# Two more landing places for raw weights in the first chunk, and two more steps whose E part is added by TensorE

## The chip, the cores and the metric

The kernel runs on one core of one Trainium2 chip. The metric is the time of one execution in microseconds (us), as the device reports it; the median of several runs is given. A core has five engines with an instruction queue each: TensorE (PE in the profile, with its weight loads as PEld), VectorE (DVE), ScalarE (ACT), GpSimd (POOL) and SyncE (SP, which here only issues transfers). The engines wait for one another through semaphores. Every engine works through its own queue in order.

## The reference, cut to what matters

```python
batch, seq, dim = (8, 3008, 256)          # x, float32
n_tokens, d_model, d_ff = (24064, 256, 1536)

X = np.fft.fft(x, axis=1)
X = np.fft.fft(X, axis=2)
x = X.real.astype(np.float32).reshape(8 * 3008, 256)

gate = 1.0 / (1.0 + np.exp(-(x @ w_gate)))   # w_gate, w_val: 256 x 1536
val = x @ w_val
return (gate * val @ w_out).astype(np.float32)   # w_out: 1536 x 256
```

The weights are created as float64.

## The kernel before, in words

The Fourier transform is done with matrix products. The transform along the features is merged into the weights: `merge` multiplies a piece of `w_gate` or `w_val` with a cosine and sine table (`ps`, 8 matmul records) and ScalarE copies the result out to `G1` and `G2` (L321, L322). The transform along the sequence gives, for each of the 8 batches, the arrays `pk`, `qk` and one row E (feature 128). So a hidden pre-activation is G1 x pk, plus or minus G2 x qk, plus a term with the row E.

The work behind that is cut into chunks of 252 sequence positions (six for a batch) and a chunk into 12 steps, one for each block of 128 hidden features. Steps are numbered through from 0; chunk 0 is steps 0 to 11. In step i of the main loop the instructions are recorded in this order, and each engine keeps its share of that order (the schedule is manual):

- `front_a(i)`: TensorE writes G1 x pk for gate and value into a PSUM bank `pf`. In the first `N1` steps it also adds the E part, a product of G2 with a tile `e0` that is zero but for its row 0 (`pf<-wqk` in the profile).
- `part(i)`: keeps that half sum in `ae`. Outside of steps `N1` to 11, ScalarE does it (L598). In steps `N1` to 11 VectorE does it and adds the E part by itself, with a per-feature factor `ge` (L601, two instructions). From step 12 on, E is put into the bank by ScalarE before the products (`seed`, L582).
- `gate_a(i - 1)` and `gate_b(i - 1)`: the sigmoids and products of the step before (ScalarE L617, L635; VectorE L622 or L619, L634, L636), and on GpSimd sums of the result, `sf` (L640). L634 is the last reader of `pf`.
- weight work of chunk 0 (below).
- `back`: from step 5 on, five of the fifteen products `po` of the output of an earlier group of three steps. A group g of three feature blocks needs `wf[:, g]`, the forms of the output weights. They are built in three portions by `forms(g)`, on GpSimd for group 0 and on VectorE after it (L357, L360), with copies by ScalarE (L364).
- `front_b(i)`: TensorE adds G2 x qk in the same bank `pf`, which therefore must have been read by `part(i)`.
- `side`: transfers and other things placed at a step by hand.

Of eight PSUM banks five hold `po`. The other three serve `pf` and `ps`, one in effect for `ps` while both are used.

In chunk 0 the weights are still being prepared. They come in 18 pieces of 512 KB, as float64, and are turned into float32 by bit operations. `weight_load(j)` starts the transfer of piece j on SP into a raw place. `weight_parts(j)` is two instructions on ScalarE (L285, L286). `weight_join(j)` is three on VectorE (L295, L296, L298) and one on GpSimd (L300). `weight_use(j)` merges the piece or, for a piece of `w_out`, queues `forms`. `merge` also issues two tiny transfers to fill `ge`. Pieces 0 to 9 (`KEEP = 10`) have places of their own. Pieces 10 to 17 use the buffer of the first batch's x (`x4`) after its last reader: three raw places in turn, so that the load of piece j + 3 waits for the join of piece j, and six places for converted pieces. The steps of joins and uses are written out by hand:

```python
    for j, i in enumerate((0, 1, 2, 3, 4, 5, 6, 7, 9), 9):      # join of piece j in step i
        if i:
            pre.setdefault(i - 1, []).append(lambda j=j: weight_parts(j))
    ...
    for j, i in enumerate((0, 0, 1, 2, 0, 3, 4, 5, 4, 6, 7, 8, 8, 8, 11), 3):   # use of piece j in step i
```

Pieces 4, 7, 11, 15, 16 and 17 are of `w_out`. Piece 11 is the last that the forms of group 1 need.

Of the kernel before, what the change touches and what calls it, by code (L numbers as in the profile page):

```python
# [7 lines left out]
F32 = mybir.dt.float32  # L8
# [73 lines left out]
def kernel(  # L82
# [13 lines left out]
    P = 128  # L96
# [10 lines left out]
    WC = 256  # L107
# [20 lines left out]
    cp = ctx.enter_context(tc.tile_pool(name="cp", bufs=2))  # L128
# [4 lines left out]
    def mm(o, l, r, start, stop):  # L133
        nc.tensor.matmul(o, l, r, start=start, stop=stop, skip_group_check=True)  # L134
# [72 lines left out]
    def table_odd():  # L207
# [9 lines left out]
        for par in range(2):  # L217
# [10 lines left out]
    jobs = [(0, 0), (1, 0), (0, 1), (1, 1), (2, 0), (0, 2), (1, 2), (2, 1), (0, 3), (1, 3), (0, 4), (2, 2),  # L228
            (1, 4), (0, 5), (1, 5), (2, 3), (2, 4), (2, 5)]
    RAW, WS = {}, {}  # L230
    shared = {}
    KEEP = 10

    def weight_load(j):


        w, c = jobs[j]
        src = (moe_w_gate, moe_w_val, moe_w_out)[w]
        src = src[2 * c * P : 2 * (c + 1) * P, :] if w == 2 else src[:, c * WC : (c + 1) * WC]
        src = src.rearrange("(c p) f -> p c f", p=P)  # L240

        def some(n, pool, tag):

            if tag not in shared:
                shared[tag] = pool.tile([P, n * WC], F32, name=f"w{tag}", tag=tag)
            return shared[tag]

        def home(j):

            if j in (0, 1, 2, 3, 5):  # L250
                if j > 2:
                    ws = some(5, pqp, "qk")[:, (j // 5) * 2 * WC : (j // 5 + 1) * 2 * WC]
                    return sp.tile([P, 4 * WC], F32, name="raw", tag="sf"), ws
                t = hp.tile([P, 6 * WC], F32, name="raw", tag="h")
                return t[:, 0 : 4 * WC], t[:, 4 * WC :]
            if j in (4, 6, 9):
                t = wf[:, {4: 1, 6: 2, 9: 3}[j]].rearrange("p m n -> p (m n)")
                return t[:, 0 : 4 * WC], t[:, 4 * WC : 6 * WC]
            t = some(10, cp, "c")
            if j == 7:  # L260
                raw = pqp.tile([P, 4 * WC], F32, name="raw", tag="pk")
                return raw, t[:, 6 * WC : 8 * WC]
            return t[:, 0 : 4 * WC], t[:, 4 * WC : 6 * WC]

        if j < KEEP:
            raw, ws = home(j)
        else:
            both = some(24, xp, "x4").rearrange("p (i n) -> p i n", n=2 * WC)
            r, i = (j - KEEP) % 3 * 2, 6 + (j - KEEP) % 6
            raw, ws = both[:, r : r + 2].rearrange("p a n -> p (a n)"), both[:, i]  # L270
        raw = raw.bitcast(I32).rearrange("p (c f w) -> p c f w", c=2, w=2)
        ws = ws.rearrange("p (c f) -> p c f", c=2)
        WS[j] = ws
        if src.dtype == F32:
            nc.sync.dma_start(out=ws, in_=src)
        else:
            RAW[j] = raw
            nc.sync.dma_start(out=raw.rearrange("p c f w -> p c (f w)"), in_=src.bitcast(I32))

    def weight_parts(j):  # L280

        if j in RAW:
            raw, ws = RAW[j], WS[j]
            lo, hi = raw[:, :, :, 0], raw[:, :, :, 1]
            nc.scalar.activation(ws, hi.bitcast(F32), AF.Abs)  # L285
            nc.scalar.activation(lo, lo.bitcast(U32), AF.Copy, scale=2.0 ** -29)  # L286
# [17 lines left out]
    def weight_use(j, other=None):  # L304
        w, c = jobs[j]
        if w == 2:
            WO[c] = WS.pop(j)
            for g in range(NG):
                if (3 * g + 2) // 2 == c:
                    parts_.extend(forms(g))  # L310
        else:
            merge(WS.pop(j), w, c, other)

    def merge(ws, g, c, other):
        cs = slice(c * WC, (c + 1) * WC)
        ps = bank("ps", other)
        for h in range(2):
            for t in range(2):
                mm(ps[:, h * WC : (h + 1) * WC], dt[:, t, h * HD : (h + 1) * HD], ws[:, t, :],
                   h == 0 and t == 0, t == 1)  # L320
        nc.scalar.copy(G2[:, g, cs], ps[:, WC : 2 * WC])  # L321
        nc.scalar.copy(G1[:, g, cs], ps[:, 0:WC])  # L322
        for f in range(c * WC // P, (c + 1) * WC // P):
            (nc.sync if c else nc.scalar).dma_start(
                out=ge[:, g, f : f + 1], in_=G2[0:1, g, f * P : (f + 1) * P])

    def forms(g):

        w = [WO[f // 2].rearrange("p f (a h j) -> p f h a j", h=2, j=TB)[:, f % 2]
             for f in range(3 * g, 3 * g + 3)]  # L330
        f = wf[:, g].rearrange("p m (a j) -> p m a j", j=TB)
        engine = nc.vector if g else nc.gpsimd

        def one(i):
            return w[i // 2][:, i % 2] if i < 6 else f[:, i - 6]

        def blocks(ij, n):

            i, j = ij[0], ij[-1]
            if i == j:  # L340
                return one(i).unsqueeze(1).to_broadcast([P, n, 4, TB])
            if i >= 6:
                return f[:, i - 6 : j - 5]
            if i // 2 == j // 2:
                return w[i // 2]
            lo = 3 * g + i // 2
            if lo % 2 == 0 and j // 2 == i // 2 + 1:
                return WO[lo // 2].rearrange("p f (a h j) -> p h f a j", h=2, j=TB)[:, i % 2]
            return None

        def sums(lo, hi):
            for x, y, op, to in W_SUMS[lo:hi]:
                n = max(len(x), len(y))
                a, b = blocks(x, n), blocks(y, n)
                op = (ALU.subtract, ALU.add)[op]
                if a is not None and b is not None:
                    engine.tensor_tensor(f[:, to - 6 : to - 6 + n], a, b, op=op)  # L357
                else:
                    for i in range(n):
                        engine.tensor_tensor(f[:, to - 6 + i], one(x[i % len(x)]), one(y[i % len(y)]), op=op)  # L360

        def copies():
            for i, (a, sign) in enumerate(W_COPIES):
                nc.scalar.mul(f[:, 11 + i], one(a), float(sign))  # L364
        return [lambda: (copies(), sums(0, 2)), lambda: sums(2, 4), lambda: sums(4, 6)]
# [204 lines left out]
        nc.sync.dma_start(out=EK[i // NFT], in_=ed[b : b + 1, k0 : k0 + n].to_broadcast([P, n]))  # L570

    PF, AP, Z = {}, {}, {}
    N1 = 5

    def seed(i):

# [7 lines left out]
    def front_a(i):  # L584
        (pk, *_), ks, _, _, fs = cut(i)
        if i < NFT:
            seed(i)
        for g in range(2):
            mm(PF[i][:, g], G1[:, g, fs], pk[:, ks], i < NFT and g == 0, True)
        for g in range(2 if i < N1 else 0):  # L590
            mm(PF[i][:, g], G2[:, g, fs], shared["qk"][:, 4 * WC : 4 * WC + CH], False, True)

    def part(i):

        pqe, ks, n, f, _ = cut(i)
        AP[i] = app.tile([P, 2, CH], F32, name="ae", tag="ae")[:, :, 0:n]
        if not N1 <= i < NFT:
            nc.scalar.activation(AP[i], PF[i], AF.Copy, scale=2.0)  # L598
# [11 lines left out]
    def gate_a(i):  # L610
# [6 lines left out]
        nc.scalar.activation(H[p][:, fh, 0:n], PF[i][:, 0], AF.Sigmoid)  # L617
        if N1 <= i < NFT:
            nc.vector.scalar_tensor_tensor(out=z[:, :, ::-1], in0=AP.pop(i), scalar=2.0, in1=PF[i],  # L619
# [116 lines left out]
    for j in range(2):  # L736
        weight_load(j)
# [3 lines left out]
    for j in range(2, 5):  # L741
        weight_load(j)
    sines = load_table(1, NQ // 2)
    next(sines)
    for j in range(5, 7):
        weight_load(j)
# [4 lines left out]
    def weight_round(*js):  # L751
        for j in js:
            weight_parts(j)
            weight_join(j)
# [24 lines left out]
        then()()  # L779
    nc.scalar.dma_start(out=ed[0:1], in_=PQE[0][2][0:1])  # L780
    nc.vector.tensor_copy(e0[0:1], PQE[0][2][0:1, 0:CH])
    weight_parts(9)
    for j in range(KEEP, KEEP + 3):
        weight_load(j)
    weight_use(2)

    per = NFT * len(chunks)
# [2 lines left out]
    def at(i, *fs):  # L790
        side.setdefault(i, []).extend(fs)


    pre, use = {}, {}
    for j, i in enumerate((0, 1, 2, 3, 4, 5, 6, 7, 9), 9):
        if i:
            pre.setdefault(i - 1, []).append(lambda j=j: weight_parts(j))
        pre.setdefault(i, []).insert(0, lambda j=j: weight_join(j))
        if KEEP <= j < len(jobs) - 3:
            at(i, lambda j=j: weight_load(j + 3))  # L800
    for j, i in enumerate((0, 0, 1, 2, 0, 3, 4, 5, 4, 6, 7, 8, 8, 8, 11), 3):
        use.setdefault(i, []).append(lambda j=j: weight_use(j))
    at(N1 - 1, lambda: nc.vector.tensor_copy(PQE[0][1][0:1, 0:CH], PQE[0][2][0:1, 0:CH]))

# [38 lines left out]
    for i in range(count):  # L843
        front_a(i)
        if N1 <= i < NFT:
            part(i)
        if i:
            gate_a(i - 1)
        if not N1 <= i < NFT:
            part(i)  # L850
# [10 lines left out]
        n = 3 if i >= count - 8 else 2 + i % 2  # L861
# [60 lines left out]
```

## Time and profile before

| | |
|---|---|
| time, median of 4 runs | 1967.46 us (1965.06 to 1969.84) |
| time of the profiled execution | 1970.47 us |
| its span, first to last instruction | 1968.6 us |
| mean granted TensorE clock | 0.992 |
| chunk 0 on TensorE, first to twelfth `pf` | 50.26 to 105.12 us |

In the profile, L134 is the line of the helper that records every matmul, so TensorE's rows are told apart by what they write and read: `pf<-pk`, `pf<-wqk` (the E part), `pf<-qk`, `ps`, `po`. `x4` behind a row is a count of records, not a tile. A row's idle time stands in brackets, with the instruction that ended it. A matmul's end is modelled and lies a little behind the next one's start, so pieces of a list are measured from start to start. Rows of the engines' timelines give start and duration in us.

### The profile page before, as it was taken

The page shows a single profiled execution, that of the slowest core. Times are in us where ns is not written, and L with a number is a line of the kernel's source. Part 1 is how long each engine was busy: PE and PEld are TensorE (multiplying, and loading weights), DVE is VectorE, ACT ScalarE, POOL GpSimd, SP SyncE. Part 2 cuts the span into 40 slices and gives each one's busy share as a digit, 9 for nine tenths or more (in the row PEclk, how much of TensorE's full clock was granted, in tenths as well). Part 3 has the DMA queues.
Part 4 walks back from the last instruction along what each step waited for, and adds up shares of the span by engine and source line. Part 5 has one row for each costly group of instructions (what it writes and reads, how often), then busy time and mean ns, then how long its engine had stood idle before and what let it go on. Part 6 is the DMA issues. An engine that isn't in the chain of part 4 may idle for free.

```text
span 1968.6 us, 34539 instructions
## 1 busy us (share of the span) xinstructions
PE 1922.0 (98%) x11252; PEld 1792.0 (91%) x11252; DVE 1569.8 (80%) x3271; ACT 1341.5 (68%) x3124; POOL 1641.2 (83%) x2851
## 2 busy tenths in 40 slices
PE   6999899999999999999999999999999999999997
PEld 4889789998999999999999999999999999999997
DVE  6888797887788877878777887788878887777777
ACT  3567656665777767776777767777677776777775
POOL 3779897997889978897889978998788996777776
PEclk8999999999999999999999999999999999999999
DMA  8361413112112120221113121221210110011011
GB/s 268 89 133 24 102 42 109 47 20 78 22 46 51 22 78 14 52 54 47 46 19 76 24 78 20 45 55 20 79 21 14 19 22 14 14 20 22 14 19 28
DMA packets 169746, 96.78 MB, mean 49 GB/s; under 512 B 133858, under 2 KB 161636, under 8 KB 167020
## 3 DMA queue, kind: packets, MB, share of 16 engines
q1 hardware_dynamic: 167596, 94.02, 20.0%
q8 instruction: 90, 1.47, 0.3%
q10 hardware_dynamic: 1940, 0.56, 0.2%
q14 instruction: 88, 0.72, 0.1%
q0 software_dynamic: 32, 0.00, 0.0%
HBM read 69.83 MB, written 46.71 MB: 59 GB/s over the span
## 4 chain that ended last, share of the span: by engine, by line
PE 89%; DVE 4%; POOL 4%; ACT 1%; DMA 1%; issue 1%; SPq 0%; DVEq 0%; ACTq 0%; POOLq 0%
PE pf L134 47%; PE po L134 39%; POOL sf L640 3%; PE ev L134 2%; PE od L134 1%; DMA x<-in_xf_dram 1%; DVE c L687 1%; DVE h L636 0%; PE ps L134 0%; DVE st L485 0%; POOL x L388 0%; ACT z L635 0%; POOL x L407 0%; POOL x L386 0%; DVE z L622 0%
## 5 line engine op out<-in xcount | busy, mean ns | idle before, releaser
L640 POOL TENSOR_TENSOR sf<-h 128x168 f32<-128x168 f32 (+1 forms) x960 | 553.6, 595 | 201.6 <-DVE h L636 201.5
L640 POOL TENSOR_TENSOR sf<-h,sf 128x168 f32<-128x168 f32 (+1 forms) x1152 | 661.9, 594 | 59.4 <-DVE h L636 59.4
L134 PE MATMUL pf<-qk,G 128*128 128x252 f32 (+1 forms) x2304 | 584.0, 376 | 7.7 <-ACT ae L598 5.6
L134 PE MATMUL pf<-pk,G 128*128 128x252 f32 (+1 forms) x2304 | 584.6, 376 | 0.0
L636 DVE TENSOR_TENSOR h<-z 128x252 f32<-128x252 f32 (+1 forms) x576 | 303.5, 527 | 329.9 <-ACT z L635 329.3
L582 ACT ACTIVATE pf<-ek,ge 128x252 f32<-128x252 f32 (+1 forms) x1128 | 531.6, 471 | 18.4
L134 PE MATMUL po<-sf,wf 128*128 128x168 f32 (+1 forms) x3072 | 530.6, 306 | 0.0
L598 ACT ACTIVATE ae<-pf 128x504 f32<-128x504 f32 (+1 forms) x569 | 335.5, 590 | 238.7 <-PE pf L134 238.2
L687 DVE TENSOR_TENSOR c<-c 128x168 f32<-128x168 f32 (+1 forms) x949 | 485.3, 542 | 5.5 <-ACT c L664 0.3
L134 PEld LDWEIGHTS pf<-pk,G 128*128 128x128 f32 x2304 | 437.0, 190 | 53.5 <-issue 2.3
L134 PEld LDWEIGHTS po<-sf,wf 128*128 128x128 f32 x3072 | 473.5, 190 | 8.3
L134 PE MATMUL po<-h,wf 128*128 128x168 f32 (+1 forms) x2688 | 476.6, 306 | 0.4 <-DVE wf L357 0.4
L134 PEld LDWEIGHTS po<-h,wf 128*128 128x128 f32 x2688 | 428.3, 190 | 17.5 <-DVE wf L357 0.6
L134 PEld LDWEIGHTS pf<-qk,G 128*128 128x128 f32 x2304 | 410.3, 190 | 35.6 <-ACT ae L598 7.6
L622 DVE TENSOR_TENSOR z<-ae,pf 128x504 f32<-128x504 f32 (+1 forms) x569 | 377.8, 664 | 21.0 <-ACT h L617 20.4
L617 ACT ACTIVATE h<-pf 128x252 f32<-128x252 f32 (+1 forms) x576 | 218.3, 379 | 159.4 <-PE pf L134 149.7
L635 ACT ACTIVATE z<-z 128x252 f32<-128x252 f32 (+1 forms) x576 | 231.6, 402 | 98.2 <-DVE z L622 77.0
L634 DVE TENSOR_TENSOR h<-h,pf 128x252 f32<-128x252 f32 (+1 forms) x576 | 232.3, 403 | 0.0
L640 POOL TENSOR_TENSOR sf<-sf 128x168 f32<-128x168 f32 (+1 forms) x192 | 111.6, 581 | 15.1
L640 POOL TENSOR_TENSOR sf<-sf,h 128x168 f32<-128x168 f32 (+1 forms) x192 | 108.0, 563 | 0.0
L134 PE MATMUL ev<-st,x 63*128 63x189 f32 (+3 forms) x372 | 79.3, 362 | 15.2 <-DVE x L388 8.6
L134 PEld LDWEIGHTS ev<-st,x 63*128 63x128 f32 (+1 forms) x372 | 65.2, 197 | 25.7 <-DVE x L388 9.0
(138 smaller groups left out, 906.7 us busy)
## 6 DMA issues: line engine op xcount, KB each, us to landing
x<-xr SPq DMA_DIRECT2D x14, 1536.0 KB
out_dram<-os SPq DMA_DIRECT2D x380, 56.0 KB
xr<-in_xf_dram SPq DMA_DIRECT2D x14, 768.0 KB
xr<-in_xf_dram SPq DMA_DIRECT2D x35, 256.0 KB
ek<-ed SPq DMA_DIRECT2D x39, 126.0 KB
out_dram<-os SPq DMA_DIRECT2D x288, 7.0 KB
st<-in_stab_dram SPq DMA_DIRECT2D x4, 1111.9 KB
x<-in_xf_dram SPq DMA_DIRECT2D x2, 1512.0 KB
```

The source lines that it names most:

```text
L134: nc.tensor.matmul(o, l, r, start=start, stop=stop, skip_group_check=True)
L582: nc.scalar.activation(PF[i][:, g], EK[i // NFT], AF.Copy, scale=ge[:, g, f : f + 1])
L598: nc.scalar.activation(AP[i], PF[i], AF.Copy, scale=2.0)
L617: nc.scalar.activation(H[p][:, fh, 0:n], PF[i][:, 0], AF.Sigmoid)
L622: nc.vector.tensor_tensor(z[:, :, ::-1], AP.pop(i), PF[i], op=ALU.subtract)
L634: nc.vector.tensor_tensor(h[:, fh, 0:n], h[:, fh, 0:n], PF.pop(i)[:, 1], op=ALU.mult)
L635: nc.scalar.activation(z[:, 0], z[:, 0], AF.Sigmoid)
L636: nc.vector.tensor_tensor(h[:, fh, n:], z[:, 0], z[:, 1], op=ALU.mult)
L640: nc.gpsimd.tensor_tensor(block(p, dst), block(p, a), block(p, b), op=(ALU.subtract, ALU.add)[op])
L687: engine.tensor_tensor(t[:, dst * R : (dst + 1) * R], *v, op=(ALU.subtract, ALU.add)[op])
```

## The change

- The raw places of pieces 10 to 17 become five: three in `x4`, and two in a new tile `wm`. That tile is the second buffer of the pool `cp`, which the results of an output chunk (`c`) use from the end of chunk 0 on. Pieces 10 and 11 are loaded into `wm`. The load of piece j + 5 follows the join of piece j.
- Piece 9 is fully converted ahead of step 0, and the first half of piece 10 too. Step 0 has the join of piece 10, step 1 that of 11 and step 2 that of 12. Step 3 has none. From piece 13 (step 4) on, the joins stay where they were.
- Piece 11 is used in step 3 and not in step 4, so the forms of group 1 lie in steps 3, 4 and 5, and not in 4, 5 and 6.
- `N1` is 7: TensorE adds the E part in steps 0 to 6, and ScalarE's `part` stays until step 6. The copy of E into row 0 of `qk` (L803), which the `qk` products behind it use, moves from step 4 to step 6.

The changed file has five more lines from L271 on.

```diff
         else:
             both = some(24, xp, "x4").rearrange("p (i n) -> p i n", n=2 * WC)
-            r, i = (j - KEEP) % 3 * 2, 6 + (j - KEEP) % 6
-            raw, ws = both[:, r : r + 2].rearrange("p a n -> p (a n)"), both[:, i]
+            r, ws = (j - KEEP) % 5, both[:, 6 + (j - KEEP) % 6]
+            if r < 2:
+                if r == 0:
+                    shared["more"] = shared.get("more") or cp.tile([P, 10 * WC], F32, name="wm", tag="c")
+                raw = shared["more"][:, r * 4 * WC : (r + 1) * 4 * WC]
+            else:
+                raw = both[:, 2 * r - 4 : 2 * r - 2].rearrange("p a n -> p (a n)")
...
-    N1 = 5
+    N1 = 7
...
-    weight_parts(9)
-    for j in range(KEEP, KEEP + 3):
+    for j in range(KEEP, KEEP + 5):
         weight_load(j)
+    weight_round(9)
+    weight_parts(10)
     weight_use(2)
...
-    for j, i in enumerate((0, 1, 2, 3, 4, 5, 6, 7, 9), 9):
+    for j, i in enumerate((0, 1, 2, 4, 5, 6, 7, 9), 10):
         if i:
             pre.setdefault(i - 1, []).append(lambda j=j: weight_parts(j))
         pre.setdefault(i, []).insert(0, lambda j=j: weight_join(j))
-        if KEEP <= j < len(jobs) - 3:
-            at(i, lambda j=j: weight_load(j + 3))
-    for j, i in enumerate((0, 0, 1, 2, 0, 3, 4, 5, 4, 6, 7, 8, 8, 8, 11), 3):
+        if KEEP <= j < len(jobs) - 5:
+            at(i, lambda j=j: weight_load(j + 5))
+    for j, i in enumerate((0, 0, 1, 2, 0, 3, 4, 5, 3, 6, 7, 8, 8, 8, 11), 3):
         use.setdefault(i, []).append(lambda j=j: weight_use(j))
```

## The prediction

> **What bounds the kernel now.** I read the page's chain of waits first, then TensorE's timeline of chunk 0, then the timelines of the engines that the waits there name.
>
> ```profile
> PE 1922.0 (98%) x11252; PEld 1792.0 (91%) x11252; DVE 1569.8 (80%) x3271; ACT 1341.5 (68%) x3124; POOL 1641.2 (83%) x2851
> PE 89%; DVE 4%; POOL 4%; ACT 1%; DMA 1%; issue 1%; SPq 0%; DVEq 0%; ACTq 0%; POOLq 0%
> ```
>
> TensorE is the bound: busy 98% of the span and 89% of the chain. Anything taken off another engine counts only where TensorE waits for it, and every added matmul counts in full. The edits lie in steps 0 to 7, so TensorE's own list there is what matters (start, us, line, shape, count, and in brackets the idle time before and who ended it):
>
> ```profile
> 68.41 1.01 PE L134 MATMUL pf<-pk,G 128*128 128x252 f32 x4
> 69.25 1.01 PE L134 MATMUL pf<-wqk,G 128*128 128x252 f32 x4
> 70.11 1.89 PE L134 MATMUL ps<-wf,dt 128*128 128x256 f32 x8
> 71.83 1.01 PE L134 MATMUL pf<-qk,G 128*128 128x252 f32 x4
> 72.68 1.01 PE L134 MATMUL pf<-pk,G 128*128 128x252 f32 x4
> 75.14 1.97 PE L134 MATMUL ps<-wx,dt 128*128 128x256 f32 x8 [1.44 <-ACT G L322]
> ...
> 81.29 1.97 PE L134 MATMUL ps<-wx,dt 128*128 128x256 f32 x8 [0.68 <-ACT G L322]
> ...
> 86.89 1.97 PE L134 MATMUL ps<-wx,dt 128*128 128x256 f32 x8 [0.51 <-POOL sf L640]
> ...
> 95.82 1.01 PE L134 MATMUL pf<-pk,G 128*128 128x252 f32 x4
> ...
> 103.38 1.95 PE L134 MATMUL pf<-qk,G 128*128 128x252 f32 x4 [2.00 <-DVE ae L601]
> ```
>
> The first four lines are step 4, 72.68 begins step 5, 95.82 begins step 9. From 53 to 73.5 us TensorE never waits. In steps 5, 6 and 7 it waits once each, always in front of the weight product ps. Step 10 has a wait of its own. Now who is late (DVE, then ACT):
>
> ```profile
> 72.08 0.76 DVE L295 TENSOR_SCALAR wx<-wx 128x512 f32<-128x512 f32 x1
> 72.88 0.65 DVE L296 TENSOR_SCALAR wx<-wx 128x512 int32<-128x512 int32 x1
> 73.56 1.67 DVE L298 SCALAR_TENSOR_TENSOR wx<-wx 128x512 int32<-128x512 int32 x1
> ...
> 75.76 1.39 DVE L360 TENSOR_TENSOR wf<-wf,wx 128x128 f32<-128x128 f32 x1
> 77.07 0.62 DVE L803 COPY qk<-ek 1x252 f32<-1x252 f32 x1
> 77.61 0.85 DVE L601 SCALAR_TENSOR_TENSOR ae<-ek,ge,pf 128x252 f32<-128x252 f32 x2
> ```
> ```profile
> 73.23 0.68 ACT L285 ACTIVATE wx<-wx 128x512 f32<-128x512 f32 x1 [1.72 <-DMA wx<-in_moe_w_val_dram]
> ...
> 74.36 0.36 ACT L321 COPY G<-ps 128x256 f32<-128x256 f32 x1
> ```
>
> Two causes. ACT waits 1.72 us for piece 14, whose load left SP only at 69.27, when POOL had freed its raw place; behind it in ACT's order stands the copy that empties ps of step 4, and the next ps needs that bank. And DVE has, in step 4, a join (72.08 to 75.15) and the first forms of group 1 (to 77.07), then the copy and the E part: without a pause from 70.40 to 79.4. ACT's z (L635) waits for DVE's L619, and the next copies out of ps stand behind that: 0.68 and 0.51.
>
> **The change part by part, TensorE.** Start to start, from rows with no wait before: pk 0.85 (68.41 to 69.25), E part 0.85, ps 1.73, five products po 1.43 (88.69 to 90.12), qk 0.85. Steps 5 to 8 without waits would be 4 x (0.85 + 1.73 + 1.43 + 0.85) = 19.44. They took 95.82 - 72.68 = 23.14, so 3.70 is lost: 2.63 of idle in the three brackets, about 0.16 more at each (a row's end lies 0.16 behind the next start: 1.01 against 0.85), and 0.6 in slower rows just behind the waits. The change adds the E part to steps 5 and 6: 2 x 0.85 = 1.70 on the bound engine, nothing hides it. If all three waits go: 19.44 + 1.70 = 21.14, that is 2.00 less. If none goes: 1.70 more.
>
> **Do the waits go?** DVE's rows, start to start: gate (L622, L634, L636) 0.59 + 0.34 + 0.34 = 1.27; a join beside a busy POOL 2.31 (80.89 to 83.20); forms of group 1: 1.92, 1.03 (79.86 to 80.89) and 0.96 (85.46 to 86.42); E part 0.78; copy 0.54. New loads against TensorE's step: step 3, 1.27 + 1.92 = 3.2 (of 4.28); step 4, 1.27 + 1.03 + 2.31 = 4.6 (4.28); step 5, 1.27 + 0.96 + 2.31 = 4.5 (5.71); step 6, 1.27 + 2.31 + 0.54 = 4.1 (5.71); step 7, 0.78 + 1.27 + 2.31 = 4.4 (4.86). Before, step 4 alone asked for 1.27 + 3.07 + 1.92 + 0.54 + 0.78 = 7.6. The debt of 0.3 after step 4 is paid in step 5. If that cover failed, a late L634 would hold the pf bank of the second next step, 5 us later: not reached. ACT gets back 2 x 0.49 (L598) in steps 5 and 6; its parts, 2 x 0.57, and the copy out of ps follow with over 2 us to spare before the next ps. The copy of E into qk (now behind step 6) waits for TensorE's last qk of that step; queued behind it on DVE is only the E part of step 7, which needs pk of step 7 anyway (0.85 later, the copy takes 0.54): nothing.
>
> **Loads.** Pieces 10 and 11 need no longer wait for the folded x (SP stood until 48.42) and go out behind piece 9, whose issue ended at 31.67. Pieces 12 to 14 leave at 48.42 as 10 to 12 did, so 14 is there 20 us before ACT wants it; 15 to 17 wait for POOL's joins of 10, 11, 12. On SP they push only the tiny ge transfers, first read by DVE in step 7 (near 85) and sent before 74. What lies ahead of 10 and 11 is the risk:
>
> ```profile
> 45.20 0.68 ACT L285 ACTIVATE wc<-raw 128x512 f32<-128x512 f32 x1 [3.50 <-DMA raw<-in_moe_w_out_dram]
> ```
>
> This is piece 7, and from here DVE runs without a pause to the E copy (L781) that TensorE waits for at 52.05. Pieces 5, 6, 7 left SP within 1.5 us (26.23 to 27.74) and were there at 37.5, 40.1 and 45.2: they came in the order of issue, not together. So I take 0 for two transfers behind them; the other end is sharing, 1.05 MB at 280 GB/s = 3.7 us later, one for one on the path. Earlier than now is excluded, since nothing ahead of them is removed. The Trainium skill, DMA: Bandwidth & Descriptors, section on queues, rings and completion order, says that an engine takes its ring's descriptors in order but that completions need not follow it; by that, too, the sum keeps 0 but not for certain.
>
> Piece 9 is converted where it was (DVE 51.92 to 53.43). Piece 10 follows: ACT 49.35 to 50.5, before the 53.20 at which it next waits; DVE 53.4 to 55.0 (alone) or 56.4 (slowed by POOL, as L296's 1.40 at 68.14 against 0.43 at 59.19), before the 56.68 at which it next works; POOL 1.25, which moves the forms of group 0 to end at 59 to 61, needed at 76. If 10 lands late, ACT has until 52.4 before qk of step 0 moves. Zero, up to 1 for a late landing. A rule that speaks against this: the skill's SBUF — State Buffer, two separate sides, says that VectorE and GpSimd lock each other out of a shared port pair for a whole instruction. By it each of six moved DVE instructions could stand behind one of POOL's 0.73 to 1.3 us; by the rows only some do, and 1.7 us of idle time (55.0 to 56.68) takes that.
>
> **Step 10.** In step 9 DVE still has the join of piece 17 and forms of group 2 (99.14 to 102.47), the same instructions in the same order. The wait of 2.00 stays, and behind it the clock falls: the windows of 2 us from 102 show 0.88, 0.50, 0.77, and eight pf matmuls take 3.64 in place of 1.70, 1.94 lost. I take no change; the ends are 4.1 gained (wait, 0.16 and slow matmuls all gone) and 2 lost (one more such drop).
>
> **Sum.** +1.70 - 3.70 = -2.00. The profiled execution took 1970.47 (span 1968.6), 3.0 above the median of the runs; its like would be 1968.5, and the median goes from 1967.46 to 1965.5. A measurement of this kernel tells about 0.2% (3.9 us) from no change, so the likeliest case lies within that.
>
> **Rivals.** *Stalls of step 10 go as well.* DVE comes to step 8 about 0.9 us earlier (join 16 kept it until 92.8, pk was there at 92), and the clock drops on a wait of 2.00 but not on one of 1.44; a slightly shorter or differently placed wait may keep it. -2.0 with 1.9 to 4.1 more: 1961.4 to 1963.5. Against it: DVE waited for TensorE at 96.87, so nothing older than step 9 is in this wait. *The early loads hold up piece 7*: slower. 3.7 us at 45.20 go to TensorE's wait at 52.05; that wait, 0.8 now, is then over 4, and the clock falls as in step 10 (1.9). 3.7 + 1.9 - 2.0 = +3.6; with 10 late as well, up to 1 more: 1971.1 to 1972.1. It decides from 2 us of delay. Against it: the order of landings. *The waits move instead of going*, to another bank or engine, and the matmuls stay: up to +1.7, 1969.2.
>
> **How the numbers follow.** Likeliest 0.44 (0.04 of it below 1963.5), step 10 too 0.31 (0.29 below), loads hold up piece 7 0.17 (0.14 above 1971.4, smaller delays within), waits move 0.08 (0.02 above). Faster 0.33, same 0.51, slower 0.16. The likeliest alone: 1963.0 to 1967.5. The range reaches to the one rival's 1961.0 and most of the way to the other: 1970.5.
>
> **What would show it.** Right: 28 matmul rows of the E part (pf<-wqk) in place of 20, no wait before ps in steps 5 to 7, ACT without a wait for wx in step 4, pk of step 9 near 93.8, and the wait of 2 us in step 10 still there. Wrong: piece 7 on ACT later than 45.2, a wait at 52 above 1 us, a new wait of pf for a bank or of DVE for ge, or step 10 without its slow matmuls.

## The result, and the profile after

The changed kernel takes 1964.56 us (median of 48 runs, 1961.99 to 1973.79). The kernel before, on the same chips, takes 1967.17 us (72 runs, 1963.89 to 1977.36). The ratio is 0.9984, with a 95% interval of 0.9978 to 0.999: 2.0 to 4.3 us less, 3.1 in the middle (the two medians lie 2.61 apart). That is below the 0.2% that the prediction called no change, with the interval reaching a little past it. The profiled execution of the changed kernel took 1964.89 us (span 1963.0, mean granted clock 0.994).

Its page, TensorE's share of the span and of the chain of waits:

```profile
PE 1919.9 (98%) x11260; PEld 1792.4 (91%) x11260; DVE 1568.3 (80%) x3267; ACT 1342.9 (68%) x3126; POOL 1639.3 (84%) x2851
PE 90%; DVE 4%; POOL 2%; DMA 2%; ACT 1%; issue 0%; DVEq 0%; ACTq 0%; SPq 0%; POOLq 0%
```

TensorE has 8 instructions more, the two E parts. Its busy time is lower all the same, 1919.9 for 1922.0 us: its matmuls ran at a higher granted clock (0.994 for 0.992 in the mean). That is a first hint that part of what the two profiled executions differ by has nothing to do with the edits. TensorE's timeline of chunk 0 after: the wait of step 0, the rows from the first `pf` product of step 5 (72.25) to that of step 9 (93.35), and the wait of step 10 (`ae` is what VectorE's E part writes):

```profile
51.61 1.12 PE L134 MATMUL pf<-wqk,G 128*128 128x252 f32 x4 [0.79 <-DVE wqk L786]
...
72.25 1.01 PE L134 MATMUL pf<-pk,G 128*128 128x252 f32 x4
73.10 1.01 PE L134 MATMUL pf<-wqk,G 128*128 128x252 f32 x4
73.95 1.89 PE L134 MATMUL ps<-wx,dt 128*128 128x256 f32 x8
...
79.65 1.89 PE L134 MATMUL ps<-wx,dt 128*128 128x256 f32 x8
...
84.50 1.89 PE L134 MATMUL ps<-wx,dt 128*128 128x256 f32 x8
...
93.35 1.01 PE L134 MATMUL pf<-pk,G 128*128 128x252 f32 x4
...
100.91 1.83 PE L134 MATMUL pf<-qk,G 128*128 128x252 f32 x4 [1.99 <-DVE ae L606]
```

No `ps` has a bracket any more. Step 5 to step 9 is 93.35 - 72.25 = 21.10 us; it was 23.14. The wait of step 10 is as long as before, and the stretch behind it too (from the first `pf` of step 9 to that of step 12 13.32 us in both).

ScalarE after. The first row is piece 7 before step 0, the second is the join half of step 4, where the wait for piece 14 stood:

```profile
44.77 0.67 ACT L290 ACTIVATE wc<-raw 128x512 f32<-128x512 f32 x1 [4.43 <-DMA raw<-in_moe_w_out_dram]
...
71.05 0.66 ACT L290 ACTIVATE wx<-wx 128x512 f32<-128x512 f32 x1
```

Piece 7 is there at 44.77 (45.20 before) although two more transfers were queued behind it. Counted from its issue on SP (27.23 after, 27.74 before) it took 17.54 us, and 17.46 before. VectorE after, in steps 3 and 4:

```profile
66.98 0.62 DVE L365 TENSOR_TENSOR wf<-wc,wx 128x128 f32<-128x128 f32 x1
67.53 0.82 DVE L365 TENSOR_TENSOR wf<-wx 128x128 f32<-128x128 f32 x1
68.27 0.54 DVE L365 TENSOR_TENSOR wf<-wf,wc 128x128 f32<-128x128 f32 x1
68.73 1.38 DVE L365 TENSOR_TENSOR wf<-wf,wx 128x128 f32<-128x128 f32 x1
70.03 0.67 DVE L627 TENSOR_TENSOR z<-ae,pf 128x504 f32<-128x504 f32 x1
70.62 0.40 DVE L639 TENSOR_TENSOR h<-h,pf 128x252 f32<-128x252 f32 x1
71.17 0.61 DVE L641 TENSOR_TENSOR h<-z 128x252 f32<-128x252 f32 x1 [0.15 <-ACT z L640]
71.71 0.76 DVE L362 TENSOR_TENSOR wf<-wx,wf 128x256 f32<-128x256 f32 x1
```

The first forms of group 1 now stand in step 3 without a join, and take 3.05 us (66.98 to 70.03). From one gate's L627 to the next, VectorE takes 4.73, 4.92 and 6.03 us in steps 3 to 5 (65.30, 70.03, 74.95, 80.98), and 4.45 in step 6 up to the E part of step 7 (85.43): 20.1 in all, against 20.0 of TensorE (4.28 + 4.28 + 5.70 + 5.70). So VectorE has lost 1.1 us against TensorE after step 4 and 1.4 after step 5, and 0.2 is left by step 7; TensorE waits for none of it.

Where the rest of the difference between the two profiled executions lies can be read by laying the same rows side by side. The first row of step 0's E part is 0.44 earlier after (51.61 for 52.05), the first `pf` of step 9 2.47 (93.35 for 95.82), so 2.03 comes from between. The wait at 208 us is 2.70 earlier (205.45 for 208.15), the next long one 4.33 (226.65 for 230.98), and the end 5.6. The 1.63 between those two waits, which lie outside the edited steps, is a clock that fell behind the first wait in one execution and not in the other. Windows of TensorE (the first four columns of numbers: window, its length, busy time with count, granted clock), first before, then after:

```profile
204.00:208.00 4.00, 1.30 (x10) 1.00 0.95 226
208.00:212.00 4.00, 3.85 (x13) 0.67 1.04 215
```
```profile
201.30:205.30 4.00, 1.39 (x10) 1.00 0.93 225
205.30:209.30 4.00, 3.85 (x21) 1.00 1.06 217
```

The waits are 2.85 and 2.76 us long, in the same place. Behind the next wait it is the other way round (2.11 us before, and the clock stays at 1.00 in the 4 us from 230; 2.16 us after, and it falls to 0.68 in the 4 us from 226), and the 1.63 is given back: at the first `pf` of step 49 the lead is 2.68 (232.41 for 235.09). It grows again in the transform work between steps 64 and 65, from 3.19 (279.13 for 282.32) to 5.06 (293.39 for 298.45): behind a wait of 2.62 us in both, the clock of the kernel before falls to 0.58 (294 to 298) and that of the changed one stays at 1.00 (291 to 295). Such differences are the noise that the medians carry; the traces show only the 2.0 us of steps 5 to 8 as the change's.

### The profile page after: what moved, and what is told of

Read it like the earlier page. It is cut to its first block, busy times and chain, and to the rows that moved or that the text cites. A ratio compares the mean times of both kernels' runs of the same rounds, so it can differ in the third digit from the quotient of the medians.

```text
span 1963.0 us, 34554 instructions
## 1 busy us (share of the span) xinstructions
PE 1919.9 (98%) x11260; PEld 1792.4 (91%) x11260; DVE 1568.3 (80%) x3267; ACT 1342.9 (68%) x3126; POOL 1639.3 (84%) x2851
## 4 chain that ended last, share of the span: by engine, by line
PE 90%; DVE 4%; POOL 2%; DMA 2%; ACT 1%; issue 0%; DVEq 0%; ACTq 0%; SPq 0%; POOLq 0%
PE pf L134 48%; PE po L134 39%; POOL sf L645 2%; DVE c L692 1%; PE ev L134 1%; PE ps L134 1%; DMA st<-in_stab_dram 1%; PE od L134 1%; DMA ge<-G 1%; DVE h L641 1%; DVE z L627 0%; DVE st L490 0%; ACT z L640 0%; POOL x L412 0%; DMA raw<-in_moe_w_val_dram 0%
## 5 line engine op out<-in xcount | busy, mean ns | idle before, releaser
L627 DVE TENSOR_TENSOR z<-ae,pf 128x504 f32<-128x504 f32 (+1 forms) x571 | 379.1, 664 | 18.6 <-ACT h L622 18.2
L640 ACT ACTIVATE z<-z 128x252 f32<-128x252 f32 (+1 forms) x576 | 231.6, 402 | 86.0 <-DVE z L627 70.8
```

Source lines behind the costliest of these rows:

```text
L627: nc.vector.tensor_tensor(z[:, :, ::-1], AP.pop(i), PF[i], op=ALU.subtract)
L640: nc.scalar.activation(z[:, 0], z[:, 0], AF.Sigmoid)
```

## The experiments

The theory, T: in steps 5 to 7 TensorE waited for VectorE's surplus of step 4 and for piece 14, and the change takes both away and pays 1.70 us for it. Rivals: only one of the two parts counts; the early loads cost something; step 10 depends on what comes before it. The stretches below run from one step's first `pf` to another's in the profiled execution. They are finer than the medians: the runs spread by several us from one execution to the next.

**The places alone, and seven steps alone.** The first kernel is the changed one with TensorE adding the E part in five steps, the second the kernel before with seven.

```diff
-    N1 = 7      # the changed kernel
+    N1 = 5
```
```diff
-    N1 = 5      # the kernel before
+    N1 = 7
```

> The whole change but N1, which stays at 5: VectorE adds the E part in steps 5 and 6 again. Measure: from pk of step 5 to pk of step 9 (before 23.14 us, after 21.10). Theory (early loads and spread joins take the waits away; the two E parts on TensorE cost 2 x 0.85 bare and buy little): VectorE is asked for 5.9 us in step 5 (0.54 + 0.78 + 1.27 + 0.96 + 2.31) against 4.86 of TensorE, so one wait of about 0.9 us before ps stays in step 6 or 7: 19.44 + 0.9 = 20.3, and the kernel is about 0.8 us faster than the changed one. Rival (N1 = 7 is what takes the waits away): they come back, 23.1, and the kernel is about 2 us slower than the changed one.

> The kernel before with N1 = 7 alone; loads, joins and forms as before. Theory (two causes, the late load of piece 14 and the crowded VectorE): 1.70 us of matmuls are added, VectorE's share of the waits goes, but ScalarE still waits some 1.7 us for piece 14 in step 4, of which the E part of step 5 now hides 0.85: 21.14 + 0.75 = 21.9 us from pk of step 5 to pk of step 9, about 1.2 us faster than before. Rival A (the E part alone is enough): 21.1. Rival B (it buys nothing): 23.14 + 1.70 = 24.8, 1.7 us slower than before.

The places alone: step 5 to step 9 took 21.86 us, 1.28 less than before; ratio 1.0001 (0.9984 to 1.0017). This lies between the two expectations. Two waits stayed:

```profile
85.33 1.97 PE L134 MATMUL ps<-wx,dt 128*128 128x256 f32 x8 [0.69 <-ACT G L327]
91.66 1.96 PE L134 MATMUL ps<-wx,dt 128*128 128x256 f32 x8 [0.69 <-ACT G L327]
```

ScalarE's order before the first of these shows whom the copy out of the bank stands behind:

```profile
83.12 0.41 ACT L640 ACTIVATE z<-z 128x252 f32<-128x252 f32 x1 [3.52 <-DVE z L627]
83.44 0.67 ACT L290 ACTIVATE wx<-wm 128x512 f32<-128x512 f32 x1
84.01 0.67 ACT L291 ACTIVATE wm<-wm 128x512 int32<-128x512 uint32 x1
84.56 0.36 ACT L326 COPY G<-ps 128x256 f32<-128x256 f32 x1
84.81 0.38 ACT L327 COPY G<-ps 128x256 f32<-128x256 f32 x1
```

A gate of VectorE that is late (L627) holds ScalarE's L640. Behind that stand the two halves of a piece and then the copies that empty `ps`, and TensorE waits for those. So the bracket names ScalarE, but the cause is VectorE, whose E part (L606, 0.85 us) lies ahead of the gate. With seven steps alone the stretch took 21.93 us (21.9 expected), 1.21 less than before; ratio 0.9986 (0.9971 to 1.0). One wait of 0.58 was left, in step 5, and it is piece 14's: ScalarE waits for its load, and the copies out of `ps` stand behind that (78.94 to 79.56).

```profile
77.79 0.70 ACT L285 ACTIVATE wx<-wx 128x512 f32<-128x512 f32 x1 [1.69 <-DMA wx<-in_moe_w_val_dram]
```
```profile
79.72 1.97 PE L134 MATMUL ps<-wx,dt 128*128 128x256 f32 x8 [0.58 <-ACT G L322]
```

So each part alone gives 1.2 to 1.3 us and both give 2.04: they overlap by 0.45. The two E parts are not the price of the change; put on TensorE, they pay for themselves: 1.70 us are spent, 1.70 + 0.76 = 2.46 come back. No kernel here has the early loads without the joins spread, so how the 1.28 divides between the two is not shown.

**Six steps.** Changed kernel, `N1 = 6`.

> The changed kernel with N1 = 6: TensorE adds the E part in step 5, VectorE in step 6. Measured so far from pk of step 5 to pk of step 9: before 23.14 us, N1 = 5 with the rest of the change 21.86, the change 21.10. Theory A (waits fall off once VectorE is past the forms of group 1, so the seventh E part is one too many): about 20.5 to 20.8, kernel 0.3 to 0.6 us faster than the changed one. Theory B (each E part buys as much waiting as it costs or more): 21.1 to 21.6, same or slower by up to 0.5 us. The kernel as a whole will be the same within what can be measured; the trace decides.

21.90 us, more than either theory had; ratio 1.0004 (0.999 to 1.0017). Waits of 0.31 (`qk` of step 6) and 0.69 (`ps` of step 7) remain. The sixth step's E part thus changes nothing against five (21.86), the seventh is worth 0.80. Here the moved E part paid only where no late gate was left between steps 5 and 7.

**The forms of group 1 put back to steps 4 to 6.**

```diff
-    ... enumerate((0, 0, 1, 2, 0, 3, 4, 5, 3, 6, 7, 8, 8, 8, 11), 3):
+    ... enumerate((0, 0, 1, 2, 0, 3, 4, 5, 4, 6, 7, 8, 8, 8, 11), 3):
```

> The changed kernel with the forms of group 1 in steps 4, 5 and 6 again, each beside a join. Theory (it is the total asked of VectorE over steps 4 to 7 that matters, and 0.85 us of E part in steps 5 and 6 give room): step 4 asks 1.27 + 1.92 + 2.31 = 5.5 of 4.28 and leaves a debt of 1.2 to 2.3, step 5 4.6 and step 6 5.1 of 5.71 pay it; 21.1 us from pk of step 5 to pk of step 9, kernel the same as the changed one. Rival (the forms beside a join are what made ScalarE's copy out of ps late): 0.7 us or more of waits before ps in steps 5 to 7.

21.11 us without a wait in steps 5 to 7; ratio 1.0001 (0.9986 to 1.0016). In the trace this part of the change is worth nothing beside the others. The run also shows something else. Its wait of step 10 is 1.99 us, as after, but the matmuls behind it stay fast: 11.94 from step 9 to step 12 and not 13.32. The windows, after first, then this kernel:

```profile
100.00:102.00 2.00, 1.09 (x3) 0.79 0.26 80
102.00:104.00 2.00, 2.00 (x6) 0.50 0.29 100
```
```profile
102.00:104.00 2.00, 2.00 (x10) 1.00 0.26 87
104.00:106.00 2.00, 2.00 (x13) 1.00 0.61 178
```

**The early loads ahead of pieces 7 to 9.** If the early loads cost nothing because pieces land in the order of issue, they must cost something when they are issued first.

```diff
-    for j in range(7, KEEP):
+    for j in (10, 11, 7, 8, 9):
         weight_load(j)
...
-    for j in range(KEEP, KEEP + 5):
+    for j in range(KEEP + 2, KEEP + 5):
```

> The changed kernel with the loads of pieces 10 and 11 issued ahead of pieces 7, 8 and 9, not behind. Theory (transfers of SP's queue come in the order of issue): two transfers, 1.05 MB at 280 GB/s, push piece 7 on ScalarE from 44.8 us to about 48.5, and TensorE's first E part from 51.6 to about 55.3; with slow matmuls behind the longer wait the kernel is 4 to 6 us slower than the changed one. Rival (the transfers share the engines, so order hardly matters, and the early loads already cost): piece 7 comes within 1 us of 44.8.

```profile
47.40 0.66 ACT L290 ACTIVATE wc<-raw 128x512 f32<-128x512 f32 x1 [7.32 <-DMA raw<-in_moe_w_out_dram]
```
```profile
50.60 3.59 PE L134 MATMUL ps<-raw,dt 128*128 128x256 f32 x8 [2.89 <-ACT a L494]
```

Piece 7 comes 2.63 us later (47.40 for 44.77). TensorE waits 2.89 us before step 0, for a copy of ScalarE (`a`, L494) that stands behind piece 7 in its order; its `ps` then runs at about half speed, and step 1 begins 3.16 us later (58.30 for 55.14). The one execution took 1968.96 us. So the order of issue counts: two pieces ahead of piece 7 cost 2.6 us, and behind it, where the change puts them, they cost nothing. That is less than the 3.7 of two whole transfers, and why is open; when pieces 10 and 11 themselves land is not seen, as no engine waits for them.

**The join of piece 17 moved out of step 9**, to step 7 behind that of piece 16.

```diff
-    ... enumerate((0, 1, 2, 4, 5, 6, 7, 9), 10):
+    ... enumerate((0, 1, 2, 4, 5, 6, 7, 7), 10):
...
-        pre.setdefault(i, []).insert(0, lambda j=j: weight_join(j))
+        pre.setdefault(i, []).insert(j == 17, lambda j=j: weight_join(j))
```

> The changed kernel with the join of piece 17 in step 7, behind that of piece 16, and not in step 9. Theory (the wait of 2 us in step 10 is that join's place, and the slow matmuls are the wait's): VectorE is asked for 6.7 us in step 7 (4.86 on TensorE) and 3.4 in step 8 (4.86), the debt is paid there; step 9 asks 3.1 of 3.13. From pk of step 9 to pk of step 12, 13.32 us in the changed kernel, it takes 9.4 to 10.0; the kernel is 3.3 to 3.9 us faster than the changed one, near 1961. Rival: the wait only moves, to ps of step 8 (ScalarE has two more instructions before its copy) or qk of step 9: less than 1 us is gained.

Ratio 0.9976 (0.9963 to 0.999). The wait of step 10 is gone: step 9 to step 12 took 10.35 us, 2.97 less than after, though more than the 9.4 to 10.0 expected. But step 5 to step 9 took 22.22, 1.12 more, with waits of 0.39 and 0.16, and the sum of the two is 1.85 less: between the theory's 3.3 or more and the rival's less than 1. The join causes the stall of step 10, and its work is paid in part where it is put.

**The same join in step 6**, its converted form in a free part of the new tile.

```diff
+        if j == 17:
+            ws = shared["more"][:, 8 * WC :]
...
-    ... enumerate((0, 1, 2, 4, 5, 6, 7, 9), 10):
+    ... enumerate((0, 1, 2, 4, 5, 6, 7, 6), 10):
```

As in the run before this one, the join is recorded behind that of the other piece of its step. This kernel and that with both moves have the forms of group 1 in steps 4 to 6, as before the change.

> The changed kernel with the join of piece 17 in step 6, behind that of piece 15, its converted form in a free part of wm. With the join in step 7 the wait of step 10 was gone (10.35 us from pk of step 9 to pk of step 12, 13.32 in the changed kernel), but 1.1 us came back as waits before ps of step 7 and qk of step 8. Theory (step 6 has 5.71 us for 6.4 asked, and step 7 pays the rest): 21.1 to 21.4 us from pk of step 5 to pk of step 9 and 9.4 to 10.4 from there to pk of step 12; the kernel 2.9 to 3.9 us faster than the changed one. Rival (two joins in one step delay ScalarE's copy out of ps wherever they stand): 22.2 and 10.4, as with step 7.

Ratio 0.9982 (0.9969 to 0.9996). 22.33 us from step 5 to step 9, with a wait of 0.83 before the `qk` products of step 7, and 9.70 from step 9 to step 12: the theory's second figure and the rival's first. Net 2.4 us less in the two stretches.

**The join of piece 8 behind the E copy**, in the changed kernel. TensorE's wait in step 0 is for that copy (`wqk`), and the join of piece 8 lies ahead of it on VectorE.

```diff
-    for then, js in zip(evacuate, ((2, 3), (4,), (5,), (6,), (7,), (8,))):
+    for then, js in zip(evacuate, ((2, 3), (4,), (5,), (6,), (7,), ())):
...
-    weight_round(9)
+    weight_round(8, 9)
```

> The changed kernel, with nothing but the join of piece 8 moved behind the E copy before step 0. Theory (TensorE's wait between steps 0 and 1 is for VectorE's join of piece 8 ahead of the E copy): 4.28 us instead of 5.33 from the first pk of step 0 to that of step 1; from step 5 to step 9 21.1 and from step 9 to step 12 13.3 (or 11.9 where the matmuls behind the wait of step 10 stay fast); median 1.0 us below the changed kernel, near 1963.5. Rival (the join is only later, and the first use of piece 8's forms waits for it): the 1.0 us come back as a wait in steps 1 to 4, median 1964.5.

1963.99 us; ratio 0.9979 (0.9964 to 0.9993). Step 0 took 4.28 us and had no wait; step 5 to step 9 took 21.46, 0.36 more; the wait of step 10 stayed, with fast matmuls behind it this time (11.93). In four other executions in which TensorE came late to step 0 (53.4 us or later) that wait was missing or short as well, 4.27 to 4.37 us, without this edit.

What decides there is how far TensorE's first `pf` lies behind piece 7. In every kernel without the edit VectorE's E copy starts 6.0 to 6.1 us behind piece 7's first instruction on ScalarE. TensorE's first `pf` came 5.06 and 5.04 us behind that instruction before and after, and waits; in the four late executions it came 6.00 to 6.63 behind it. In this run it came 6.61 behind (50.09 and 43.48), so the wait would have been missing without the edit, and this run does not show the edit's worth. Two of the other kernels that have it do (both moves together, and the last of this section): with `pf` 4.55 us behind piece 7, the copy starts 4.05 and 4.06 behind it, and step 0 has no wait.

The 0.36 goes back to that lead. VectorE's gate of step 6 stands at 81.08, as after (80.98), while TensorE's step 6 begins 0.77 earlier (77.18 for 77.95); ScalarE's copy out of `ps` ends at 83.86, and the `ps` of step 7 starts 1.13 behind its `pf` (82.88 and 84.01), not 0.85.

**Both moves together.** The join of piece 17 in step 6 and that of piece 8 behind the copy.

> As with the join of piece 17 in step 6, and the join of piece 8 behind the copy of E that TensorE's first E part waits for (0.79 us in the changed kernel). Theory (VectorE comes to that copy 1.5 to 2 us earlier, so the wait goes and nothing else is late, as piece 8 is used in step 3): no wait before the first pf<-wqk, 0.8 to 0.95 us faster than the other, 3.7 to 4.9 us faster than the changed kernel. Rival (piece 9 and 10 behind it make ScalarE or VectorE late in step 0): a new wait before qk of step 0 or ps of step 1.

1963.77 us; ratio 0.9974 (0.9962 to 0.9986), a span of 1959.9. The wait in step 0 is gone (4.28 us) and the rival's new wait in steps 0 and 1 did not come. But that nothing else would be late was wrong: step 5 to step 9 took 23.25 us with this wait, 0.92 more than with the join of piece 17 alone moved to step 6; 9.70 us behind:

```profile
88.28 1.12 PE L134 MATMUL pf<-qk,G 128*128 128x252 f32 x4 [1.34 <-DVE ae L608]
```

**Piece 17 in step 8, piece 8 behind the copy.**

```diff
-    ... enumerate((0, 1, 2, 4, 5, 6, 7, 9), 10):
+    ... enumerate((0, 1, 2, 4, 5, 6, 7, 8), 10):
```

> The run with the join of piece 8 behind the E copy, and beside it the join of piece 17 one step earlier than in the changed kernel, in step 8, where VectorE has no other join. Theory (a join costs TensorE only what VectorE's step holds above TensorE's): steps 0 to 1 4.28 us; from step 5 to step 9 21.1 to 21.5 us; VectorE's forms and E part of step 9 end some 1.7 us later than before, of which 0.4 is slack, so a wait of 0.8 to 1.3 us in step 9 in place of the 2.0 in step 10, and from step 9 to step 12 10.3 to 11.0 us instead of 13.3. Median 3.3 to 4.0 us below the changed kernel, near 1961. Rival (the wait of step 10 only moves ahead by a step, at its full size of 2.0 us and with slow matmuls behind it): from step 9 to step 12 12 to 13.3 us, median near 1963.5, as with the join of piece 8 alone.

1962.93 us against 1965.55 of the kernel before on that chip; ratio 0.9987 (0.9978 to 0.9996), a span of 1959.7. The three stretches took 4.28, 21.80 and 11.42 us. The wait is 1.25 us and in step 9, as the theory said, but the second stretch is 0.3 and the third 0.4 longer than expected:

```profile
95.31 1.12 PE L134 MATMUL pf<-qk,G 128*128 128x252 f32 x4 [1.25 <-DVE ae L606]
```

**One join for each of steps 0 to 7**, alone and with piece 8 behind the copy. In both kernels the converted form of piece 16 comes into piece 10's place one step too early, so that the product of step 5 reads piece 16's magnitudes and not piece 10: these two kernels do not compute the reference.

> The joins of pieces 10 to 17 stand in steps 0 to 7, one for each step, the converted form of piece 17 lies in the last part of the new tile, and the forms of group 1 are written in steps 4 to 6. Theory (what counts for a step is whether VectorE's work of it, gate, join, forms and E part, stays under TensorE's): VectorE has some 3.6 us of work in step 3, 5.5 to 6.1 in step 4, 4.6 in step 5, 5.1 in step 6 and 4.4 in step 7, against 4.28, 4.28, 5.71, 5.71 and 4.86 us of TensorE; step 4's surplus is covered by the lead of earlier steps. Nothing waits in steps 5 to 8 but 0.3 us at the most: from the first pk of step 5 to that of step 9 21.1 to 21.4 us. The wait of step 10 goes: from step 9 to step 12 9.4 to 9.7 us instead of 13.32. Median 3.3 to 3.9 us below the changed kernel, near 1961. Rival (the work of a join only moves the wait to the step it is put in, as with piece 17's join in steps 6 or 7): a wait of 0.8 to 1.3 us in steps 4 to 7, 22.2 to 23.2 us from step 5 to step 9, median near 1962 to 1963.

> As the run with the joins one for each step, and the join of piece 8 behind the E copy before step 0. Theory: from the first pk of step 0 to that of step 1 4.28 us instead of 5.33, and steps 5 to 12 as in the run with the joins alone: 21.1 to 21.4 and 9.4 to 9.7 us; median 4.3 to 4.9 us below the changed kernel, near 1960. Rival (VectorE has no time left for it, what was ahead of step 0 comes back in steps 4 to 7, as it did in the run with both moves, where step 6 took 6.05 us): 22.3 to 23.3 us from step 5 to step 9, median near 1961.5 to 1962.5.

Both theories missed: 1969.18 us, ratio 1.0008 (0.9994 to 1.0021), and 1967.91, ratio 1.0005 (0.9993 to 1.0018). Step 9 to step 12 took 9.70 in both, but step 5 to step 9 26.91 and 26.65:

```profile
78.38 3.08 PE L134 MATMUL ps<-wx,dt 128*128 128x256 f32 x8 [3.85 <-ACT wx L292]
```
```profile
77.36 0.41 ACT L642 ACTIVATE z<-z 128x252 f32<-128x252 f32 x1 [2.14 <-DVE z L629]
77.68 0.65 ACT L292 ACTIVATE wx<-wm 128x512 f32<-128x512 f32 x1
```

The product of step 5 has become a reader of what ScalarE writes for piece 16 (L292), ScalarE stands behind its L642 (two lines further down in this file than L640 after), and that stands behind VectorE's L629, which comes at 76.66. VectorE had a join (71.76 to 74.08) and the first forms of group 1 (74.08 to 76.66) in step 4, 6.8 us from gate to gate and not the 5.5 to 6.1 expected. How much of the 3.85 the late VectorE would cost without the shared place was not tried.

All kernels side by side. Stretches in us of the profiled execution; the last column is the ratio less one, times 1967.5 us, with its interval.

| kernel | step 0 to 1 | 5 to 9 | 9 to 12 | 0 to 12 | runs against before, us |
|---|---|---|---|---|---|
| before | 5.32 | 23.14 | 13.32 | 58.88 | |
| places alone | 4.36 | 21.86 | 13.32 | 56.65 | +0.2 (-3.1 to +3.3) |
| seven steps alone | 4.37 | 21.93 | 11.94 | 55.34 | -2.8 (-5.7 to 0) |
| six steps | 4.36 | 21.90 | 13.32 | 56.68 | +0.8 (-2.0 to +3.3) |
| forms at 4 | 5.32 | 21.11 | 11.94 | 55.47 | +0.2 (-2.8 to +3.1) |
| loads ahead (one execution) | 4.27 | 21.11 | 13.32 | 55.81 | |
| **the changed kernel** | 5.33 | 21.10 | 13.32 | 56.86 | -3.1 (-4.3 to -2.0) |
| 17 in step 7 | 4.56 | 22.22 | 10.35 | 54.24 | -4.7 (-7.3 to -2.0) |
| 17 in step 6 | 5.31 | 22.33 | 9.70 | 54.45 | -3.5 (-6.1 to -0.8) |
| 8 behind the copy | 4.28 | 21.46 | 11.93 | 54.78 | -4.1 (-7.1 to -1.4) |
| both moves | 4.28 | 23.25 | 9.70 | 54.34 | -5.1 (-7.5 to -2.8) |
| 17 in step 8, 8 behind the copy | 4.28 | 21.80 | 11.42 | 54.61 | -2.6 (-4.3 to -0.8) |
| joins in 0 to 7 | 5.33 | 26.91 | 9.70 | 59.04 | +1.6 (-1.2 to +4.1) |
| joins in 0 to 7, 8 behind the copy | 4.27 | 26.65 | 9.70 | 57.73 | +1.0 (-1.4 to +3.5) |

The five kernels between the changed one and the last two rows shorten chunk 0 by 2.1 to 2.6 us more than the change does, in the trace. Not all of that is theirs: where only piece 8 is moved, 1.4 of the 2.1 is the clock behind step 10's wait, and with piece 17 in step 7, 0.77 of the 2.6 is step 0, where that kernel changes nothing and TensorE came 5.91 us behind piece 7. Against the kernel before, all five intervals lie below zero. By the runs none of them can be told from the changed kernel, as every interval overlaps its own, so which version is the fastest stays open.

## Why the prediction was right

**The sum.** 19.44 bare and 1.70 for two E parts made 21.14; 21.10 was measured. Against the runs, -2.0 was forecast and -3.1 (-4.3 to -2.0) measured: the forecast is at the edge of the interval. The trace places 2.03 in steps 5 to 8 and, before the rows of 208 us, 0.67 more; the rest of the profiled execution's 5.6 is mostly the clock behind the unchanged wait near 294 us. That the runs gained more than 2.0 is therefore not shown to be the change's.

**The waits go.** Right, all three, and for the two causes named: the experiments with one part each give 1.28 and 1.21, with VectorE's late gate left over in the one and piece 14 in the other.

**VectorE's walk.** The mechanism was right, the sizes were not. The prediction summed 3.2 + 4.6 + 4.5 + 4.1 = 16.4 us for steps 3 to 6 and saw a debt of 0.3 after step 4, paid in step 5; VectorE took 20.1, and the debt was 1.1 after step 4, 1.4 after step 5 and was paid in step 6. The terms at fault are the gate, taken as 1.27 (from L627 to the next job it measured 1.68 in steps 3 and 4, 2.06 and 1.93 in steps 5 and 6, with a wait of 0.15 to 0.29 for ScalarE's L640 inside that was left out), the first forms, taken as 1.92 (3.05), and the two other portions, taken as 1.03 and 0.96 (1.37 and 1.65). It cost nothing here, since the cover was enough, but that was in part luck: ScalarE's copy out of `ps` was to be done with over 2 us to spare, and it ended 1.1, 1.9 and 0.7 us ahead of the `ps` of steps 5, 6 and 7 (72.81 for 73.95, 77.73 for 79.65, 83.76 for 84.50). It did cost in an expectation: with the places alone the stretch was to take 20.3 us, and the two waits that were left made it 21.86.

**Loads.** Right. Piece 7 came at 44.77. The price of the rival was too high: two pieces ahead are worth 2.6 us, not 3.7. And its path was another: the delay reached TensorE by ScalarE's copy in front of the `ps` of step 0, not at the E copy.

**Piece 10 before step 0.** Right: ScalarE took it at 48.92 without a wait, and VectorE's join ended at 55.50. That lies between the prediction's two values. Its L301 took 1.41 us there (53.45 to 54.86), where 0.43 was taken alone: GpSimd's L305 had begun at 53.21 and ended at 54.57. The Trainium skill's SBUF — State Buffer, two separate sides, says that whichever of the two has the shared port pair first holds it for its whole instruction (on VectorE's side for its two-port modes or two inputs in SBUF); an end 0.29 us behind GpSimd's agrees with that. The two other instructions of the join had no GpSimd instruction begun ahead of them, and took 0.42 and 0.69.

**Step 10.** Right for this pair of executions: 13.32 before and after. The rival that had it go as well needed something older than step 9 in that wait. There is nothing older: VectorE idles for TensorE ahead of the E part of step 9, 0.32 us before and 0.66 after, and only taking piece 17's join out of step 9 made the 2.00 go away. But the prediction took the slow matmuls behind a wait of 2.00 as given. They are not (see below), and they cost 1.4 by comparison with the three executions that kept the clock, not 1.94. The gain for all of step 10's stall, put at 4.1, measured 3.6 (13.32 to 9.70).

## What to carry to other kernels

Count the other engines' work for each step of the bound engine, with rows taken from the same company (beside a busy GpSimd, not alone), and follow a late gate through the in-order queue to the copy that frees a PSUM bank: the bracket names the last in that line, not its cause. Extra work on the bound engine can pay when it takes an instruction from ahead of such a gate, but here only once the gate was no longer late for another reason: the sixth E part was worth nothing and the seventh 0.8 us. A join taken out of a stalled step took the stall away, but part of it came back as waits where the join was put (1.2 of 3.6 us in step 6). And before a missing wait is put down to an edit, see whether the waiting engine came late in that execution.

## What the runs showed of the hardware

- **The clock behind one and the same wait.** The wait of step 10 was 1.99 or 2.00 us in eight kernels' profiled executions. In five of them (before, after, places alone, six steps, loads ahead) the granted clock then fell to 0.50 in a window of 2 us, and the stretch took 13.32; in three (seven steps alone, forms at 4, 8 behind the copy) it stayed at 1.00, and the stretch took 11.93 or 11.94. The edits do not sort these groups. The Trainium skill, TensorE: Matmul & The Clock Gate, Part 1, gives an idle window of about 3.4 us for the fall and says that the window is free-running, so that the number of slow matmuls at a kernel's start varies from run to run. A variation was seen here behind a wait too; the length was not, as the clock fell after 2.0 us of idle time. Other waits show the same: behind 2.85 us it fell (before) and behind 2.76 it did not (after), behind 2.11 it did not (before) and behind 2.16 it did (after).
- **The start.** TensorE begins step 0 between 48.4 and 57.3 us. A wait of 7 to 9 us ahead of its products near 22 us is in every execution (8.63 before, 7.96 after) and does not sort them. What differs is a wait behind it, for the table `st`: 2.67, 3.23 and 2.23 us in the two latest executions (57.26 and 55.80) and the one at 53.41, and at most 1.39 in the others. The row of the second:

```profile
48.48 1.54 PE L134 MATMUL ev<-st,x 126*128 126x377 f32 x2 [3.23 <-DMA st<-in_stab_dram]
```

This row is of the kernel with seven steps alone, whose loads are those of before. In the profiled executions of before and after that wait is 0 and 0.43 us. In those three it is as long as the change's 2.0 us or longer, and what sets it was not tried.
